# A recurrence and an expert layer on one core: the floor of the decay product inside its scan, a product moved to GpSimd, and one step in three rebalanced between TensorE and VectorE

## The chip, the cores and the metric

The kernel runs on one core of a Trainium2 chip. The metric is the device time of one execution in microseconds (us), taken as the median of several runs. The kernel before took 398.53 us (three runs, 396.94 to 400.71).

## What is computed

A decayed linear attention (4 batches, 8 heads, 768 tokens, 48 channels) feeds a layer of eight experts, of which each token takes one.

```python
for t in range(S):
    kt, vt, rt, wt = (k[:, :, t], v[:, :, t], r[:, :, t], w[:, :, t])
    cur = np.einsum('bhd,bhe->bhde', u[None] * kt, vt)
    y[:, :, t] = np.einsum('bhd,bhde->bhe', rt, state + cur)
    state = wt[:, :, :, None] * state + np.einsum('bhd,bhe->bhde', kt, vt)
...
e_idx = np.argmax(x @ w_gate, axis=1)
...
    h = np.maximum(x[mask] @ w1[e], 0.0)
    out[mask] = gate_w[mask, None] * eom[mask, e, None] * (h @ w2[e])
```

The term `cur` is the **own term** below: what a token takes from its own key and value, through u.

## The kernel before

**Two parts.** The recurrence is cut into 24 chunks of 128 tokens, six to a batch. It fills the first 152 us or so. Then come the experts, whose products fill TensorE almost to the end. The weights of the experts are fetched from about 125 us on, into five buffers.

**A unit** is the decay work for one or two chunks; there are 13 (units 0 and 1 have one chunk, unit u from 2 on has chunks 2(u-1) and 2(u-1)+1). All of it is on VectorE: `suffix` (L343) scans the decays w backwards into `sf` (L351), takes the whole product of a chunk from its first column, not less than FLOOR (2^-100), into `prods` (L357), and writes its reciprocal into the start of the next scan (L359). `times_rk` (L325) multiplies r and k into `rkp` (L331), for the own term. `prefix` (L361) scans forward into `pp` (L367). `scale_r` (L378) multiplies r by `pp` (L382) and `scale_k` (L371) k by `sf` (L375), both **in place** in the tile `rks`. So `scale_r` of a unit may only start when its `times_rk` has read r.

**A chunk.** TensorE forms the scores (`scores`, `pat`, L451). ScalarE copies them out, one instruction for each of two halves (L469); GpSimd puts the causal mask on each half (L475). In one chunk of three, from chunk 6 on, VectorE does copy and mask of one half in one instruction (L466). `outputs` (L536) sums masked scores times v (L550) and r times the old state (L558) in PSUM tile `py`, of which there is one buffer. `state` (L503) adds the old state to the new products on TensorE through a product with the identity (L509), or leaves that to VectorE (`tmp`, L525); ScalarE then scales the sum by `prods` into the next state (L530). `own` (L489) makes the own term `dv` on ScalarE (L494). It is added in one of two ways: by TensorE, through a product with the identity (L562), after which VectorE sums the gate columns (L593) and ScalarE copies the rows (L594, which waits for L593); or by VectorE (`sums`, L598 to L601, four instructions), which then frees `py` itself.

**Order.** Every engine works through its instructions in program order. That order comes from a table O of due times, in chunks. The entries `eu`, `ps` and `po` say where work goes, by u or k modulo 3: a positive `eu` puts `times_rk` on GpSimd, a positive `ps` adds the old state on TensorE, a positive `po` adds the own term on TensorE. `po` counts from chunk 6 on, and both end at chunk 17.

**After the recurrence** the rows of the last chunk are stored, and the next weights are queued behind that store on SyncE; the last tokens are routed, and GpSimd gathers their rows.

Of the kernel before, what the change touches and what calls it, by code (L numbers as in the profile page):

```python
# [17 lines left out]
ALU = mybir.AluOpType  # L18
# [33 lines left out]
FLOOR = 2.0 ** -100  # L52
# [1 line left out]
LIMIT = 2.0 ** 20  # L54


O = {'turnl': 0.22, 'fetch2': 1.36, 'fetch1': 1.35, 'fetch0': 1.34, 'list': 0.84, 'count': 0.83, 'match': 0.305, 'known': 0.839, 'read': -0.7, 'late': 0.46, 'vgm': -1.61, 'vgt': -1.07, 'vg': -1.618, 'vgo': -0.703, 'score': -1.649, 'so0': -1.336, 'so1': -1.268, 'mask0': -0.673, 'mask1': -0.914, 'key': -1.529, 'ko': -1.232, 'own': -0.619, 'state': -0.175, 'sto': -0.036, 'out': 0.238, 'sums': 0.397, 'const': 2.67, 'ra': 0.72, 'rd': 0.15, 'rb': 1.282, 'lr': [0, 22], 'lp': 2, 'pf': 0, 'rn': 5, 'rz': .45, 'rdz': 0.05, 'sumz': 0.323, 'sc': 2.6, 'scw': 0.9, 'open': -0.6, 'fetch': 3.4, 'up': 2.11, 'lo': 2.5, 'turn0': 4.3, 'turno0': 4.32, 'turn1': 4.301, 'turno1': 4.33, 'turn2': 4.302, 'turno2': 4.34, 'warm': 15, 'sc1': 1.55, 'sc2': [1.55, 1.55, 3.4, 3.4, 4.4, 4.4], 'ra2': .55, 'rd2': .07, 'rb2': 1.0, 'sc3': 5.939, 'lw': -5.962, 'lrk': -4.5, 'lv': -4.4, 'sfx': -3.687, 'pfx': -3.529, 'sk': -2.206, 'sr': -2.924, 'ruk': -3.598, 'min': 0.313, 'ed': 1, 'eu0': -1, 'ek0': -1, 'er0': -1, 'em00': -1, 'em01': 1, 'eu1': -1, 'ek1': -1, 'er1': -1, 'em10': 1, 'em11': 1, 'eu2': -1, 'ek2': -1, 'er2': -1, 'em20': 1, 'em21': 1, 'ps0': -1, 'po0': 1, 'ps1': 1, 'po1': -1, 'ps2': 1, 'po2': 1, 'ps3': 1, 'po3': 1, 'ps4': 1, 'po4': -1, 'sa0': 1, 'sa1': -1, 'sa2': 1, 'du': -1.35, 'raws': -.35, 'w0': 4, 'w1': 0, 'wt0': 0.945, 'wn0': 0, 'wt1': -1.03, 'wn1': 6, 'wt2': -0.602, 'wn2': 0, 'wt3': 1.387, 'wn3': 0}


@with_exitstack  # L60
def tile_rwkv_moe(ctx: ExitStack, tc, rkT, wz, v_tok, vT, r_raw, k_raw, v_raw,
                  w_raw, u, uT, wg, wgb, wog, w12, out):
    nc = tc.nc
    const = ctx.enter_context(tc.tile_pool(name="const", bufs=1))
# [86 lines left out]
    raws, pieces, nth = {}, {}, {}  # L151
# [165 lines left out]
    def load_rk(u):  # L317

        marks("lrk", u)
        k, n = units[u]  # L320
        rks[u] = pa.tile([P, 2 * NP, 2, C], F32, tag="rks", name="rks", bufs=RKB)
        nc.sync.dma_start(rks[u][:, 0:n * NP].rearrange("p n k t -> p (n k t)"),
                          rkT[k // 2, :, k % 2 * NP * 2 * C:][:, 0:n * NP * 2 * C])

    def times_rk(u, i=0):  # L325

        marks("rk", u, "lrk", i=i)
        n = parts(u, i) if u else slice(0, NP)
        if i == 0:
            rkp[u] = pa.tile([P, 2 * NP, C], F32, tag="rkp", name="rkp", bufs=2)  # L330
        engine(O["eu%d" % (u % 3)]).tensor_tensor(  # L331
            out=rkp[u][:, n], in0=rks[u][:, n, 0], in1=rks[u][:, n, 1], op=ALU.mult)

    def parts(u, i):

        if u == SPLIT:
            return slice(i * NP, (i + 1) * NP)
        return (slice(0, 2), slice(2, NP))[i] if u == 0 else slice(0, units[u][1] * NP)

    def flat(t, n):  # L340
        return t[:, n].rearrange("p n t -> p (n t)")

    def suffix(u, i=0):  # L343

        n = parts(u, i)
        marks("sfx", u, "lw", i=i)
        if u > 1:
            mark(("sfx", u, "dp", i), ("pfx", sum(units[u - 2]) - 1))
        if i == 0:
            sfs[u] = pa.tile([P, 2 * NP, W1C], F32, tag="sf", name="sf", bufs=2)  # L350
        nc.vector.tensor_tensor_scan(  # L351
            out=flat(sfs[u], n)[:, ::-1],
            data0=wts[u][:, n.stop * W1C:n.start * W1C:-1],
            data1=flat(dsx, n)[:, ::-1],
            initial=0.0, op0=ALU.mult, op1=ALU.add)
# [15 lines left out]
    def scale_k(u, i=0):  # L371
        n = parts(u, i)
        marks("sk", u, "sfx", "rk", i=i)
        kh = rks[u][:, n, 1]
        engine(O["ek%d" % (u % 3)] if u else -1).tensor_tensor(  # L375
            out=kh, in0=kh, op=ALU.mult, in1=sfs[u][:, n, 1:W1C])

    def scale_r(u, i=0):  # L378
        n = parts(u, i)
        marks("sr", u, "pfx", "rk", i=i)  # L380
        rh = rks[u][:, n, 0]
        engine(O["er%d" % (u % 3)] if u else -1).tensor_tensor(  # L382
            out=rh, in0=rh, op=ALU.mult, in1=pps[u][:, n, 0:C])
# [50 lines left out]
    def vgate_out(k):  # L434
# [547 lines left out]
    load_w(2)  # L982
    load_v(1)
    load_rk(2)
    nc.vector.memset(dsx, 0.0)
    nc.vector.memset(dsx[:, :, C], 1.0)
    nc.vector.memset(dpx[0], 0.0)
    make_identity(nc, ident)
    nc.gpsimd.memset(dpx[1], 0.0)
    constants()  # L990
    suffix(0, 0)
    prefix(0, 0)
    suffix(0, 1)
# [519 lines left out]
```

## Time and profile before

| what | value |
|---|---|
| median of 3 runs | 398.53 us (396.94 to 400.71) |
| profiled execution, its own time | 400.15 us |
| its span, first to last instruction | 398.6 us |
| TensorE busy in the span | 377.1 us (95%) |
| VectorE busy | 315.9 us (79%) |
| ScalarE busy | 245.7 us (62%) |
| GpSimd busy | 209.0 us (52%) |
| granted TensorE clock, mean | 0.993 |

Busy is the time in which at least one instruction of an engine ran. An instruction that waits inside its own duration, as for a port, counts as busy there. PE is TensorE's products, PEld its weight loads, DVE VectorE, ACT ScalarE, POOL GpSimd, SP SyncE. A row of the timeline gives start, duration, engine, line, operation, out<-in with shapes, and in brackets the idle time ahead of it with what ended it; "x2" is two instructions in a row.

### The profile page before, as it was taken

Reading aid. Unit: us, or ns where it says so; the run is one execution under the profiler, and the core shown is the slowest. Engines: PE = TensorE matmul, PEld = TensorE weight load, DVE = VectorE, ACT = ScalarE, POOL = GpSimd, SP = SyncE. Lnnn points to the kernel's source line nnn. Section 1 sums busy time; section 2 is a strip of 40 time slices with the busy share of each in tenths; the row PEclk is TensorE's granted clock in tenths of the full one; section 3 lists DMA queues with packets and bytes.
Section 4 is the critical chain, followed back from the end, with each engine's and each line's share of the span. In section 5 each row is a group of like instructions: output and inputs, shape, how many; then the busy total and the mean of one; then the engine's idle time right before and its main releaser. Section 6 shows DMA issues by size and latency. Waiting matters only on the chain.

```text
span 398.6 us, 10773 instructions
## 1 busy us (share of the span) xinstructions
PE 377.1 (95%) x4079; PEld 336.6 (84%) x4082; DVE 315.9 (79%) x616; ACT 245.7 (62%) x674; POOL 209.0 (52%) x234
## 2 busy tenths in 40 slices
PE   8899999999989998979999999999999999999992
PEld 3576788778767888879888999999999999999991
DVE  7999999999999877654777588699798798977521
ACT  1786789889797895422465485476556846666200
POOL 8614535668585585452053008617748388362723
PEclk9999999999999999999999999999999999999998
DMA  7995787998895822563449669789699798975212
GB/s 238 333 342 185 235 277 228 243 270 228 226 277 199 291 89 46 139 202 133 144 150 253 184 113 239 270 140 287 191 205 294 195 249 259 184 266 151 57 35 58
DMA packets 64936, 80.75 MB, mean 203 GB/s; under 512 B 40741, under 2 KB 49153, under 8 KB 63468
## 3 DMA queue, kind: packets, MB, share of 16 engines
q1 hardware_dynamic: 59580, 69.39, 62.3%
q0 software_dynamic: 4896, 10.34, 8.2%
q8 instruction: 34, 0.56, 0.6%
q10 hardware_dynamic: 400, 0.25, 0.2%
q14 instruction: 26, 0.21, 0.2%
HBM read 61.66 MB, written 10.30 MB: 181 GB/s over the span
## 4 chain that ended last, share of the span: by engine, by line
PE 56%; DVE 21%; issue 7%; DMA 6%; ACT 5%; POOL 2%; POOLq 1%; SPq 1%; ACTq 0%; DVEq 0%
PE ph L724 19%; PE acc L747 18%; DVE sf L351 3%; PE pat L451 3%; PE py L550 3%; DVE pp L367 3%; DMA raw<-in_w_dram 2%; PE py L562 2%; DVE wlo L172 2%; PE py L558 2%; DVE rkp L331 2%; PE pg L419 2%; DVE rks L375 2%; DMA xg<-xd,ids 2%; ACT whi L167 1%
## 5 line engine op out<-in xcount | busy, mean ns | idle before, releaser
L172 DVE TENSOR_TENSOR wlo<-raw,whi 128x768 fp32r<-128x768 f32 x64 | 64.0, 1000 | 20.9 <-ACT whi L167 20.1
L475 POOL TENSOR_SCALAR_AFFINE_SELECT a<-a 128x512 f32<-128x512 f32 x42 | 50.0, 1209 | 49.1 <-ACT a L469 49.1
L724 PE MATMUL ph<-xh,whi 128*128 128x384 f32 (+7 forms) x216 | 73.4, 340 | 0.8 <-DVE hl L730 0.4
L724 PE MATMUL ph<-xh,wlo 128*128 128x384 f32 (+7 forms) x216 | 72.8, 337 | 0.4 <-DVE wlo L172 0.4
L724 PE MATMUL ph<-xl,whi 128*128 128x384 f32 (+7 forms) x216 | 72.6, 336 | 0.2 <-DVE xl L939 0.2
L702 POOL COPY yj<-yr 112x384 uint16<-112x384 uint16 (+1 forms) x48 | 41.2, 912 | 57.6 <-DMA yr<-yp 57.6
L729 ACT ACTIVATE hh<-ph 128x384 fp32r<-128x384 f32 (+7 forms) x72 | 34.4, 479 | 48.9 <-PE ph L724 48.9
L747 PE MATMUL acc<-hh,whi 128*128 128x336 f32 (+6 forms) x168 | 58.7, 349 | 0.0
L747 PE MATMUL acc<-hl,whi 128*128 128x336 f32 (+6 forms) x168 | 58.5, 348 | 0.1
L747 PE MATMUL acc<-hh,wlo 128*128 128x336 f32 (+6 forms) x168 | 58.4, 347 | 0.0
L167 ACT CAST whi<-raw 128x768 fp32r<-128x768 f32 x62 | 51.8, 835 | 8.2 <-DMA raw<-in_w_dram 5.6
L730 DVE SCALAR_TENSOR_TENSOR hl<-ph,hh 128x384 fp32r<-128x384 f32 (+7 forms) x72 | 38.6, 538 | 17.4 <-ACT hh L729 17.3
L494 ACT ACTIVATE dv<-vt,dg 128x56 f32<-128x56 f32 x192 | 47.5, 354 | 0.4
L616 POOL DMA_INDIRECT xg<-xd,idm x28 | 30.1, 1073 | 25.6 <-issue 16.8
L675 POOL DMA_INDIRECT out_dram<-yo,idm x28 | 32.6, 1164 | 20.6 <-DVE yo L673 15.7
L724 PEld LDWEIGHTS ph<-xh,whi 128*128 128x128 f32 x216 | 40.8, 189 | 2.3 <-ACT xh L632 0.5
L724 PEld LDWEIGHTS ph<-xh,wlo 128*128 128x128 f32 x216 | 40.7, 188 | 1.4 <-DVE wlo L172 0.7
L724 PEld LDWEIGHTS ph<-xl,whi 128*128 128x128 f32 x216 | 40.7, 188 | 1.1 <-DVE xl L939 0.4
L268 POOL DMA_INDIRECT slot_table<-pair,slots x24 | 33.3, 1387 | 10.1 <-DVE lt L584 4.0
L747 PEld LDWEIGHTS acc<-hl,whi 128*128 128x128 f32 x168 | 31.9, 190 | 1.2 <-DVE hl L730 0.4
L747 PEld LDWEIGHTS acc<-hh,whi 128*128 128x128 f32 x168 | 32.1, 191 | 0.7
L747 PEld LDWEIGHTS acc<-hh,wlo 128*128 128x128 f32 x168 | 32.0, 190 | 0.7
(193 smaller groups left out, 764.4 us busy)
## 6 DMA issues: line engine op xcount, KB each, us to landing
raw<-in_w_dram SPq DMA_DIRECT2D x64, 384.0 KB
rks<-in_rkT_dram SPq DMA_DIRECT2D x11, 1024.0 KB
wts<-in_wz_dram SPq DMA_DIRECT2D x11, 516.5 KB
vt<-in_v_tok_dram SPq DMA_DIRECT2D x24, 224.0 KB
vs<-in_vT_dram SPq DMA_DIRECT2D x24, 192.0 KB
xd<-xt SPq DMA_DIRECT2D x24, 192.0 KB
wo<-in_wog_dram SPq DMA_DIRECT2D x8, 192.0 KB
rks<-in_rkT_dram SPq DMA_DIRECT2D x2, 512.0 KB
```

The lines of the kernel that those rows point to most:

```text
L167: (copy or nc.scalar.copy)(hi, raw)
L172: nc.vector.tensor_tensor(out=lo, in0=raws[e, f], in1=hi.bitcast(F32), op=ALU.subtract)
L268: nc.gpsimd.indirect_dma_start(out=tabs[i], out_offset=bass.IndirectOffsetOnAxis(ap=slots[:, i:i + 1], axis=0), in_=pair[:, i, :], in_offs ...
L475: nc.gpsimd.affine_select(out=a, in_=a, pattern=[[0, NP], [1, C]], compare_op=ALU.is_gt, fill=0.0, base=0, channel_multiplier=-1)
L494: nc.scalar.activation(out=dvs[k][:, p, o], in_=vts[k][:, p, VX * o:VX * o + VX], func=AF.Copy, scale=dgs[k][:, p, o:o + 1])
L616: nc.gpsimd.indirect_dma_start(out=xg[:, j, :], out_offset=None, in_=xd[0:rows, :], in_offset=bass.IndirectOffsetOnAxis(ap=idt[:, 2 * j:2 ...
L675: nc.gpsimd.indirect_dma_start(out=outs[view], out_offset=bass.IndirectOffsetOnAxis(ap=idt[:, 2 * j:2 * j + 1], axis=0), in_=yo, in_offset ...
L702: nc.gpsimd.tensor_copy(to[:, q], by[:, q])
L724: nc.tensor.matmul(ph[:, 0:nt], a[:, d * P:(d + 1) * P], x[:, d, 0:nt], start=k == 0, stop=k == 8)
L729: nc.scalar.activation(out=hh[:, 0:nt], in_=ph[:, 0:nt], func=AF.Relu)
L730: nc.vector.scalar_tensor_tensor(out=hl[:, 0:nt], in0=ph[:, 0:nt], scalar=0.0, in1=hh[:, 0:nt].bitcast(F32), op0=ALU.max, op1=ALU.subtract)
L747: nc.tensor.matmul(y[:, 0:nt], w[:, DM + i * P:DM + (i + 1) * P], a[:, 0:nt], start=start, stop=stop)
```

## The change

Four edits, all in the recurrence:

1. The scan `sf` takes the larger of its running product and a floor (`max` in place of `add`); the tile `dsx` holds FLOOR where it held 0. The `max` on VectorE (L357) goes; the reciprocal reads `sf`; a copy into `prods` follows, on GpSimd from unit 3 on, on VectorE before.
2. `times_rk` of units 4, 7 and 10 goes to GpSimd.
3. The own term of chunks 6, 9, 12 and 15 is added by VectorE (chunks 7, 10, 13, 16, 21, 22 and 23 were already).
4. The old state of chunks 3, 9 and 15 is added by TensorE.

```diff
-... 'eu1': -1, ... 'ps0': -1, 'po0': 1, ...
+... 'eu1': 1, ... 'ps0': 1, 'po0': -1, ...
...
-        engine(O["eu%d" % (u % 3)]).tensor_tensor(
+        engine(O["eu%d" % (u % 3)] if u > 3 else -1).tensor_tensor(
             out=rkp[u][:, n], in0=rks[u][:, n, 0], in1=rks[u][:, n, 1], op=ALU.mult)
...
-            initial=0.0, op0=ALU.mult, op1=ALU.add)
+            initial=0.0, op0=ALU.mult, op1=ALU.max)
         pc = prods[:, units[u][0] * NP + n.start:units[u][0] * NP + n.stop]
-        nc.vector.tensor_scalar(out=pc, scalar1=FLOOR, scalar2=None, op0=ALU.max,
-                                in0=sfs[u][:, n, 0])
-        nc.vector.reciprocal(dpx[u % 2][:, n, 0], pc)
+        nc.vector.reciprocal(dpx[u % 2][:, n, 0], sfs[u][:, n, 0])
+        (nc.gpsimd if u > 2 else nc.vector).tensor_copy(pc, sfs[u][:, n, 0])
...
-    nc.vector.memset(dsx, 0.0)
+    nc.vector.memset(dsx, FLOOR)
```

GpSimd around unit 4, before. The tiles a_107 to a_112 are the score halves of three chunks in turn; here a_108 and a_107 are chunk 3, a_110 and a_109 chunk 4:

```order
L475 AFFINE_SELECT a_112<-a_112 128x512
L475 AFFINE_SELECT a_111<-a_111 128x512
L475 AFFINE_SELECT a_108<-a_108 128x512
L475 AFFINE_SELECT a_107<-a_107 128x512
L475 AFFINE_SELECT a_110<-a_110 128x512
```

GpSimd at the same place, of the change:

```order
L474 AFFINE_SELECT a_112<-a_112 128x512
L474 AFFINE_SELECT a_111<-a_111 128x512
L474 AFFINE_SELECT a_108<-a_108 128x512
L358 COPY prods<-sf 128x8
L474 AFFINE_SELECT a_107<-a_107 128x512
L331 TENSOR_TENSOR rkp<-rks 128x1024
L474 AFFINE_SELECT a_110<-a_110 128x512
```

The copy of unit 4 stands between the two masks of chunk 3, and the product of unit 4 behind both. At units 7 and 10 the chunk has one mask on GpSimd, and the product stands right behind the copy.

VectorE at unit 4, before:

```order
L351 SCALAR_TENSOR_TENSOR sf<-wts,dsx 128x1032
L357 TENSOR_SCALAR prods<-sf 128x8
L359 RECIPROCAL dpx_105<-prods 128x8
L593 TENSOR_REDUCE logit<-py 128x8
L331 TENSOR_TENSOR rkp<-rks 128x1024
L367 SCALAR_TENSOR_TENSOR pp<-wts,dpx_105 128x1032
L525 TENSOR_TENSOR tmp<-pkv,st_93 128x224
L382 TENSOR_TENSOR rks<-rks,pp 128x8x128
```

VectorE there, of the change:

```order
L351 SCALAR_TENSOR_TENSOR sf<-wts,dsx 128x1032
L357 RECIPROCAL dpx_105<-sf 128x8
L592 TENSOR_REDUCE logit<-py 128x8
L366 SCALAR_TENSOR_TENSOR pp<-wts,dpx_105 128x1032
L381 TENSOR_TENSOR rks<-rks,pp 128x8x128
```

Three instructions are gone between the two scans and behind them; the last row, `scale_r`, now waits for GpSimd's product.

GpSimd at unit 12, before (a_110 and a_109 are chunk 19):

```order
L870 MEMSET xg 112x1152
L475 AFFINE_SELECT a_110<-a_110 128x512
L475 AFFINE_SELECT a_109<-a_109 128x512
L268 DMA slot_table<-pair,slots 3712x2 x2
L475 AFFINE_SELECT a_112<-a_112 128x512
```

And of the change:

```order
L869 MEMSET xg 112x1152
L474 AFFINE_SELECT a_110<-a_110 128x512
L358 COPY prods<-sf 128x8
L474 AFFINE_SELECT a_109<-a_109 128x512
L268 DMA slot_table<-pair,slots 3712x2 x2
L474 AFFINE_SELECT a_112<-a_112 128x512
```

The copy of unit 12 stands between the two masks of chunk 19, so the second of them now follows the scan of unit 12.

## Rows read from the trace of the kernel before

**Rows 1.** Busy time by stretch: span, then PE, PEld, DVE, ACT, POOL; clock, DMA.

```profile
45.00:82.00 37.00, 36.77 (x780) 30.28 (x780) 35.73 (x57) 33.65 (x123) 19.90 (x16) 1.00 0.82 248
...
138.00:152.00 14.00, 14.00 (x332) 11.78 (x329) 7.93 (x21) 13.97 (x52) 11.14 (x12) 1.00 0.25 79
```

**Rows 2.** The chain that ended last, in order of time: start us, us, what.

```profile
82.53 1.13 DVE rkp L331
...
156.54 4.42 DMA raw<-in_w_dram
```

**Rows 3.** VectorE in order of time around unit 4: start us, us.

```profile
37.43 0.17 DVE L357 TENSOR_SCALAR prods<-sf 128x8 f32<-128x8 f32 x1
37.63 0.21 DVE L359 RECIPROCAL dpx<-prods 128x8 f32<-128x8 f32 x1
...
37.84 1.22 DVE L331 TENSOR_TENSOR rkp<-rks 128x1024 f32<-128x1024 f32 x1
38.97 2.30 DVE L367 TENSOR_TENSOR_SCAN pp<-wts,dpx 128x1032 f32<-128x1032 f32 x1
41.19 0.37 DVE L525 TENSOR_TENSOR tmp<-pkv,st 128x224 f32<-128x224 f32 x1
41.47 1.31 DVE L382 TENSOR_TENSOR rks<-rks,pp 128x1024 f32<-128x1024 f32 x1
...
42.84 1.51 DVE L375 TENSOR_TENSOR rks<-rks,sf 128x1024 f32<-128x1024 f32 x1
```

**Rows 4.** ScalarE and GpSimd in order of time, scores of chunk 3.

```profile
38.33 1.08 ACT L469 COPY a<-pat 128x512 f32<-128x512 f32 x2
...
39.48 3.79 POOL L475 TENSOR_SCALAR_AFFINE_SELECT a<-a 128x512 f32<-128x512 f32 x2 [5.38 <-ACT a L469]
```

**Rows 5.** Mask's durations (ns min/median/max); GpSimd and VectorE in order of time.

```profile
L475 POOL TENSOR_SCALAR_AFFINE_SELECT a<-a x42: 628/1079/2534, 12.9 to 150.6; 128x512 f32<-128x512 f32 x42
...
84.13 2.18 POOL L475 TENSOR_SCALAR_AFFINE_SELECT a<-a 128x512 f32<-128x512 f32 x1 [2.10 <-ACT a L469]
...
83.58 2.30 DVE L367 TENSOR_TENSOR_SCAN pp<-wts,dpx 128x1032 f32<-128x1032 f32 x1
...
60.22 0.20 DVE L236 TENSOR_TENSOR sl<-rk,limit 128x48 f32<-128x48 f32 x1
...
93.76 1.55 POOL L475 TENSOR_SCALAR_AFFINE_SELECT a<-a 128x512 f32<-128x512 f32 x1
...
94.75 0.63 DVE L236 TENSOR_TENSOR sl<-rk,limit 128x48 f32<-128x48 f32 x1
```

**Rows 6.** VectorE and TensorE in order of time, own term on VectorE.

```profile
115.32 0.22 DVE L598 TENSOR_REDUCE lt<-py 128x8 f32<-128x64 f32 x1 [0.27 <-PE py L558]
...
116.46 1.25 DVE L331 TENSOR_TENSOR rkp<-rks 128x1024 f32<-128x1024 f32 x1
...
81.05 0.23 DVE L598 TENSOR_REDUCE lt<-py 128x8 f32<-128x64 f32 x1 [0.56 <-PE py L558]
...
101.58 1.15 PE L550 MATMUL py<-vt,a 128*64 128x56 f32 x32 [0.93 <-DVE xt L601]
```

**Rows 7.** Groups of instructions, 14 to 152 us; line L357 over the span.

```profile
L562 PE MATMUL py<-dv,ident 128*128 128x224 f32 x68 | 17.4, 379 | 0.0
...
L509 PE MATMUL pkv<-st,ident 128*128 128x224 f32 x26 | 7.5, 370 | 0.0
...
L530 ACT ACTIVATE st<-tmp,prods 128x56 f32<-128x56 f32 x12 | 3.1, 330 | 4.1 <-DVE tmp L525 4.1
...
L357 DVE TENSOR_SCALAR prods<-sf x15: 168/170/422, 4.5 to 130.3; 128x8 f32<-128x8 f32 x10, 128x4 f32<-128x4 f32 x3, 128x2 f32<-128x2 f32 x2
```

**Rows 8.** Routing, TensorE's outputs and GpSimd's masks of chunks 18 and 19.

```profile
123.81 0.20 DVE L203 TENSOR_TENSOR ohb<-io_m,em 128x48 bf16<-128x48 f32 x1
...
131.50 1.15 PE L550 MATMUL py<-vt,a 128*64 128x56 f32 x32 [0.33 <-ACT xt L594]
...
124.98 1.27 POOL L475 TENSOR_SCALAR_AFFINE_SELECT a<-a 128x512 f32<-128x512 f32 x2 [3.62 <-ACT a L469]
```

More of the change, by code (lines that the diff above doesn't have):

```diff
@@ L54 @@
 LIMIT = 2.0 ** 20
-O = {'turnl': 0.22, 'fetch2': 1.36, 'fetch1': 1.35, 'fetch0': 1.34, 'list': 0.84, 'count': 0.83, 'match': 0.305, 'known': 0.839, 'read': -0.7, 'late': 0.46, 'vgm': -1.61, 'vgt': -1.07, 'vg': -1.618, 'vgo': -0.703, 'score': -1.649, 'so0': -1.336, 'so1': -1.268, 'mask0': -0.673, 'mask1': -0.914, 'key': -1.529, 'ko': -1.232, 'own': -0.619, 'state': -0.175, 'sto': -0.036, 'out': 0.238, 'sums': 0.397, 'const': 2.67, 'ra': 0.72, 'rd': 0.15, 'rb': 1.282, 'lr': [0, 22], 'lp': 2, 'pf': 0, 'rn': 5, 'rz': .45, 'rdz': 0.05, 'sumz': 0.323, 'sc': 2.6, 'scw': 0.9, 'open': -0.6, 'fetch': 3.4, 'up': 2.11, 'lo': 2.5, 'turn0': 4.3, 'turno0': 4.32, 'turn1': 4.301, 'turno1': 4.33, 'turn2': 4.302, 'turno2': 4.34, 'warm': 15, 'sc1': 1.55, 'sc2': [1.55, 1.55, 3.4, 3.4, 4.4, 4.4], 'ra2': .55, 'rd2': .07, 'rb2': 1.0, 'sc3': 5.939, 'lw': -5.962, 'lrk': -4.5, 'lv': -4.4, 'sfx': -3.687, 'pfx': -3.529, 'sk': -2.206, 'sr': -2.924, 'ruk': -3.598, 'min': 0.313, 'ed': 1, 'eu0': -1, 'ek0': -1, 'er0': -1, 'em00': -1, 'em01': 1, 'eu1': -1, 'ek1': -1, 'er1': -1, 'em10': 1, 'em11': 1, 'eu2': -1, 'ek2': -1, 'er2': -1, 'em20': 1, 'em21': 1, 'ps0': -1, 'po0': 1, 'ps1': 1, 'po1': -1, 'ps2': 1, 'po2': 1, 'ps3': 1, 'po3': 1, 'ps4': 1, 'po4': -1, 'sa0': 1, 'sa1': -1, 'sa2': 1, 'du': -1.35, 'raws': -.35, 'w0': 4, 'w1': 0, 'wt0': 0.945, 'wn0': 0, 'wt1': -1.03, 'wn1': 6, 'wt2': -0.602, 'wn2': 0, 'wt3': 1.387, 'wn3': 0}
@@ new lines @@
+O = {'turnl': 0.22, 'fetch2': 1.36, 'fetch1': 1.35, 'fetch0': 1.34, 'list': 0.84, 'count': 0.83, 'match': 0.305, 'known': 0.839, 'read': -0.7, 'late': 0.46, 'vgm': -1.61, 'vgt': -1.07, 'vg': -1.618, 'vgo': -0.703, 'score': -1.649, 'so0': -1.336, 'so1': -1.268, 'mask0': -0.673, 'mask1': -0.914, 'key': -1.529, 'ko': -1.232, 'own': -0.619, 'state': -0.175, 'sto': -0.036, 'out': 0.238, 'sums': 0.397, 'const': 2.67, 'ra': 0.72, 'rd': 0.15, 'rb': 1.282, 'lr': [0, 22], 'lp': 2, 'pf': 0, 'rn': 5, 'rz': .45, 'rdz': 0.05, 'sumz': 0.323, 'sc': 2.6, 'scw': 0.9, 'open': -0.6, 'fetch': 3.4, 'up': 2.11, 'lo': 2.5, 'turn0': 4.3, 'turno0': 4.32, 'turn1': 4.301, 'turno1': 4.33, 'turn2': 4.302, 'turno2': 4.34, 'warm': 15, 'sc1': 1.55, 'sc2': [1.55, 1.55, 3.4, 3.4, 4.4, 4.4], 'ra2': .55, 'rd2': .07, 'rb2': 1.0, 'sc3': 5.939, 'lw': -5.962, 'lrk': -4.5, 'lv': -4.4, 'sfx': -3.687, 'pfx': -3.529, 'sk': -2.206, 'sr': -2.924, 'ruk': -3.598, 'min': 0.313, 'ed': 1, 'eu0': -1, 'ek0': -1, 'er0': -1, 'em00': -1, 'em01': 1, 'eu1': 1, 'ek1': -1, 'er1': -1, 'em10': 1, 'em11': 1, 'eu2': -1, 'ek2': -1, 'er2': -1, 'em20': 1, 'em21': 1, 'ps0': 1, 'po0': -1, 'ps1': 1, 'po1': -1, 'ps2': 1, 'po2': 1, 'ps3': 1, 'po3': 1, 'ps4': 1, 'po4': -1, 'sa0': 1, 'sa1': -1, 'sa2': 1, 'du': -1.35, 'raws': -.35, 'w0': 4, 'w1': 0, 'wt0': 0.945, 'wn0': 0, 'wt1': -1.03, 'wn1': 6, 'wt2': -0.602, 'wn2': 0, 'wt3': 1.387, 'wn3': 0}
```

## The prediction

> **What bounds the kernel now.** I read the busy time by stretch first. From 45 to 82 us TensorE is busy 36.77 of 37 us and VectorE 35.73 [rows 1]: two engines are full at once, and a microsecond taken from one is worth something only if the other keeps up. From 138 to 152 us VectorE has slack (7.93 of 14) and TensorE has none. The chain of waits tells which of the two decides: it runs through TensorE's steps until VectorE takes it over (the product r times k at 82.53 lies on it, [rows 2]), and is TensorE's again in the last stretch. What follows the recurrence hangs on its end: at 156.54 the chain goes through a weight transfer of 4.42 us [rows 2] that SyncE issues only behind the store of the last rows. So what the recurrence gains or loses arrives at the end in full.
>
> Two more things are to be seen. First, VectorE and GpSimd hold each other up. A mask alone takes 0.63 us; one that began at 84.13 took 2.18 and ended at 86.31, which is 0.43 after a VectorE scan that ran from 83.58 to 85.88 [rows 5]. So GpSimd stood until the scan was through and then needed 0.43 us for 512 elements. The other way, a small VectorE operation that takes 0.20 us took 0.63 beside a mask, and both ended at 95.3 to 95.4 [rows 5]. I read it so: a VectorE operation with two inputs in SBUF and a GpSimd operation that reads SBUF exclude one another, each for its whole length. Second, `scale_r` overwrites r, so it waits for the product r times k, wherever that is made.
>
> The Trainium skill, "SBUF — State Buffer", section "Who interferes with whom", says the same: a VectorE instruction with two SBUF inputs contends with a GpSimd instruction that reads SBUF, and the one that issues second blocks fully. The rows at 84.13 and 94.75 agree with it; it speaks against the second edit, and the sum below is what it would make of the time.
>
> **The change, part by part, on VectorE.**
>
> *Floor.* The `max` goes: from it to the reciprocal are 0.20 us (37.43 to 37.63, [rows 3]). Where GpSimd's mask runs then, it takes 0.42 instead of 0.17 [rows 7]; that happens in four of the units from 5 to 11 and saves 0.45 each there. Units 0 to 2 get a copy in its place: nothing. GpSimd's copy is new; a mask's 0.63 less the 0.43 it reads leaves 0.2 us for a tiny operation, my estimate. Between nothing and one whole mask (0.63) it changes little, except where a mask stands behind it (below).
>
> *Product.* VectorE loses 1.13 us for each of three (37.84 to 38.97, [rows 3]). No row shows this operation on GpSimd. It reads 2 x 1024 elements where the mask reads 512: four times 0.43 and 0.2 make 1.9 us. Lower bound: one mask alone, 0.63. Upper bound: four masks at their median under contention, 4 x 1.08 = 4.3 [rows 5]. I take 1.9, as the reading sets the hold. In that time VectorE can do nothing else here, since a scan and `scale_r` are all that come next, and both need the port or the product. So at units 7 and 10 it stands 1.9 us, whether the product gets in ahead of the scan `pp` or behind it.
>
> The Trainium skill, "GPSIMD Engine Reference", section "Performance versus the Vector engine", gives 4497 ns for a `tensor_tensor` of 2048 fp32 elements; half of that would be 2.25 us, an estimate, and the sum would grow by 0.35 for each product. No run here shows it.
>
> *Old state.* VectorE loses 0.28 us (41.19 to 41.47, [rows 3]) three times; ScalarE no longer waits for it, 4.1 us in all [rows 7].
>
> *Own term.* From the first of four instructions to the next other one are 1.14 us (115.32 to 116.46, [rows 6]), the middle of the five such places. What it replaces is one gate sum (L593): reciprocal and gate sum together take 0.21 (37.63 to 37.84, [rows 3]), of which I give it 0.14. So +1.0, four times.
>
> **Unit 4** needs its own working, as the product stands behind both masks of chunk 3. Before: `scale_r` at 41.47 [rows 3]. Now the scan ends 0.2 earlier (unit 3's floor), at 37.2; reciprocal and gate sum take 0.3, and `pp` runs 37.5 to 39.8. The two score copies, in before 38.33 to 39.41 [rows 4], come 0.3 earlier. The first mask waits for `pp` (in before it waited likewise: two masks took 3.79 us, [rows 4]) and ends at 40.2; copy 40.4; second mask 41.0; product 42.9. `scale_r` starts at 42.9: **1.4 late**, with two floors, the product and the old state already taken off.
>
> **The sum on VectorE**, from unit 3 to the routing of chunks 12 to 17 at 124 us:
>
> - up to `scale_r` of unit 4: +1.4
> - floors of units 5, 6, 8, 9 (0.45 each) and 11 (0.20): -2.0
> - units 7 and 10: -0.20 - 1.13 - 0.28 + 1.9 = +0.3 each: +0.6
> - own term of chunks 6, 9, 12, 15: +4.0
> - VectorE's waits for TensorE that a late VectorE no longer has, as 0.56 at 81.05 and 0.27 at 115.32 [rows 6], and two more: -1.4
> - `scale_k` ran 0.3 longer beside a mask (1.51 against the 1.22 of a product of the same shape, [rows 3]) in units 4, 7 and 10; the masks there now lie elsewhere: -0.9
>
> Together +1.7.
>
> **On TensorE** four chunks lose the own term, 17.4/17 = 1.02 us each, and three gain the old state, 7.5/13 = 0.58 each [rows 7]: -2.4, and some of its waits for ScalarE go. TensorE would be early, but it needs VectorE: for the routing (`ohb` at 123.81, [rows 8], is followed by TensorE's ranks and only then by the outputs of chunk 18), and for the outputs of chunk 19, which at 131.50 already waited 0.33 for the chain from VectorE's scan of unit 12 through L593 and ScalarE's copy [rows 8]. So TensorE's gain is lost in waiting. At chunk 19 there are +1.7, less unit 12's floor, 0.2: **+1.5**. Then TensorE works without a break, and the end moves by that.
>
> One wait is added there too: the second mask of chunk 19 was done at 126.25 [rows 8] and now follows the scan of unit 12, about 4 us later, the copy, and perhaps a whole VectorE operation that holds the port. It ends at about the time when the outputs start; behind it stand two routing scatters and the masks of chunk 20, which have 2 us to spare. I count it at nothing, with +1.0 as its upper end.
>
> The profiled execution, 400.15 us, would become 401.65. It lies 1.6 above the median of the runs shown, so on the median I forecast 398.53 + 1.5 = **400.0 us**.
>
> **Rivals.**
>
> *The port is shared, not held (faster).* If VectorE works on beside GpSimd's product, units 7 and 10 give -1.6 each, and only the masks delay unit 4 (+1.0). The sum is 1.0 - 2.0 - 3.2 + 4.0 - 1.4 - 0.9 = -2.5, and TensorE's own -2.4 would then be felt: 398.5 - 2.5 = 396.0. For it: GpSimd's spans are rough, and a mask is not a product. Against it: both blocked rows above. Chance 0.24.
>
> *The product is long (slower).* At 4.3 us the three products add 3 x 2.4 = 7.2 to the sum: about 407. From 2.8 us on (3 x 0.9 = 2.7 more) the kernel is slower by over 1%. For it: no row has a two-input operation on GpSimd, and masks under contention reach 2.53 us [rows 5]. Against it: that is waiting, not work. Chance 0.18, most of it near 403.
>
> *Nothing is felt,* because the weight transfer after the recurrence sets the next start: excluded by the chain, since its issue follows the last rows. The floor could also fail to save time, if the reciprocal just waits 0.42 where the `max` did; that costs 1.0 and lies inside the range.
>
> **How the numbers follow.** My forecast has 0.58 and by itself a range of 398.5 to 402.0. The faster rival reaches to 395.5, the slower one, but for its far end, to 403.5: the range is 395.5 to 403.5. About 1% is what a measurement of this kernel tells from no change: 394.5 and 402.5. Below lies only a faster rival that also keeps ScalarE's freed time: 0.12. Above lie the long product and a chunk 19 mask that is late as well: 0.18. The rest, 0.70, is within 1%.
>
> **What would show it.** GpSimd's product at 1.9 us after its port is free, never beside a two-input VectorE operation; VectorE idle some 3 us ahead of `scale_r` in unit 4 and about 2 in units 7 and 10; 1.1 us for each of the four new own terms; TensorE waiting for VectorE near chunks 13 to 19, with more idle time than before up to 131 us; the first weight transfer after the last rows at about 158 instead of 156.5 us. The prediction is wrong if VectorE's scans run on beside the product, or if TensorE's idle time shrinks.

## The result, and the profile after

The changed kernel takes 404.5 us (median of 4 runs, 403.78 to 404.67), the kernel before 397.9 us beside it (4 runs): a ratio of 1.0129, 95% interval 1.0085 to 1.0173. It is slower by 1.3%. A kernel's executions fall into a faster and a slower state, and the ratios here and below are taken in the faster one, so a ratio need not be the quotient of the two medians (1.0166 here). I had forecast 400.0 with a range up to 403.5, so 404.5 lies 1.0 us above the range. The sign of the forecast was right, the size and the mechanism were not.

| | before | after |
|---|---|---|
| median, us | 397.9 | 404.5 |
| profiled execution, us | 400.15 | 404.48 |
| span of its trace, us | 398.6 | 402.8 |
| mean granted clock | 0.993 | 0.977 |
| outputs of chunk 2 to those of chunk 18, us | 94.49 | 102.03 |

The last line is the stretch of the recurrence, from start to start, that holds nearly all that was changed; it serves as a measure below. The first view is the busy time by stretch (span, then PE, PEld, DVE, ACT, POOL; clock, DMA), which answers [rows 1]; first two stretches of the kernel before, then the changed kernel:

```profile
82.00:107.00 25.00, 23.44 (x475) 18.89 (x463) 24.66 (x42) 21.82 (x83) 16.44 (x12) 1.00 0.89 246
107.00:138.00 31.00, 29.49 (x599) 23.83 (x596) 29.77 (x55) 25.54 (x95) 20.43 (x15) 1.00 0.79 251
```

```profile
45.00:82.00 37.00, 34.91 (x745) 28.30 (x745) 36.46 (x55) 32.72 (x123) 23.02 (x19) 1.00 0.76 238
82.00:107.00 25.00, 22.24 (x414) 18.23 (x415) 23.45 (x40) 18.21 (x70) 16.57 (x14) 0.86 0.75 232
107.00:138.00 31.00, 26.83 (x506) 21.66 (x504) 26.09 (x49) 20.56 (x79) 20.28 (x17) 0.89 0.74 231
138.00:152.00 14.00, 14.00 (x312) 11.52 (x312) 11.64 (x15) 13.97 (x51) 12.41 (x10) 1.00 0.42 136
```

Up to 82 us this is as forecast: VectorE full, TensorE 1.9 us less busy than before. From 82 to 138 us it is not. VectorE, of which I expected that it would be the bound, is idle for 6.5 us there (1.6 before), and the granted clock, 1.00 in all of these stretches before, is 0.86 and 0.89. Neither VectorE nor TensorE is the bound, so I asked who is waited for. The group of TensorE's first output matmuls, 14 to 159 us (busy, mean ns | idle time ahead, and what ended it), says it in one line, first before, then after:

```profile
L550 PE MATMUL py<-vt,a 128*64 128x56 f32 x736 | 26.4, 224 | 1.8 <-DVE xt L601 0.9 <-ACT xt L594 0.5
```

```profile
L549 PE MATMUL py<-vt,a 128*64 128x56 f32 x736 | 28.0, 233 | 8.0 <-POOL a L474 6.4 <-DVE xt L600 1.0 <-ACT xt L593 0.4
```

TensorE waited 6.4 us for GpSimd's masks; in the kernel before not at all. It was in two places, chunk 11 and chunk 17. TensorE in order of time:

```profile
67.05 1.15 PE L549 MATMUL py<-vt,a 128*64 128x56 f32 x32 [0.99 <-DVE xt L600]
...
84.77 1.97 PE L549 MATMUL py<-vt,a 128*64 128x56 f32 x32 [2.34 <-POOL a L474]
86.67 1.12 PE L557 MATMUL py<-st,rks 64*64 64x56 f32 x32
87.72 1.86 PE L561 MATMUL py<-dv,ident 128*128 128x224 f32 x4
89.50 1.78 PE L450 MATMUL pat<-rks 64*128 64x128 f32 x16
...
123.25 1.96 PE L549 MATMUL py<-vt,a 128*64 128x56 f32 x32 [4.09 <-POOL a L474]
```

And GpSimd in order of time, ahead of the one and of the other:

```profile
71.09 2.36 POOL L331 TENSOR_TENSOR rkp<-rks 128x1024 f32<-128x1024 f32 x1
73.61 2.83 POOL L268 DMA_INDIRECT slot_table<-pair,slots  x1 [0.15 <-issue]
76.45 1.56 POOL L474 TENSOR_SCALAR_AFFINE_SELECT a<-a 128x512 f32<-128x512 f32 x2
78.18 1.78 POOL L268 DMA_INDIRECT slot_table<-pair,slots  x1 [0.16 <-issue]
79.97 1.77 POOL L474 TENSOR_SCALAR_AFFINE_SELECT a<-a 128x512 f32<-128x512 f32 x1
81.90 0.99 POOL L268 DMA_INDIRECT slot_table<-pair,slots  x1 [0.16 <-issue]
82.87 1.25 POOL L358 COPY prods<-sf 128x8 f32<-128x8 f32 x1
84.09 3.21 POOL L474 TENSOR_SCALAR_AFFINE_SELECT a<-a 128x512 f32<-128x512 f32 x2
...
107.60 0.19 POOL L358 COPY prods<-sf 128x8 f32<-128x8 f32 x1 [1.41 <-DVE sf L351]
...
118.77 0.65 POOL L474 TENSOR_SCALAR_AFFINE_SELECT a<-a 128x512 f32<-128x512 f32 x1
119.35 1.25 POOL L358 COPY prods<-sf 128x8 f32<-128x8 f32 x1
120.56 2.63 POOL L474 TENSOR_SCALAR_AFFINE_SELECT a<-a 128x512 f32<-128x512 f32 x1
```

From the product at 71.09 on GpSimd has no free moment up to 87.3 us, apart from some 0.15 us ahead of each scatter (the rows DMA_INDIRECT): product, scatter, two masks, scatter, first mask of chunk 11, scatter, copy, second mask (the first 0.62 us of the row at 84.09; the rest of that row is a mask of chunk 12). Only the second mask lets TensorE go on. At chunk 17 it is the same chain, and the mask there is held as well. Who holds copy and mask is seen on VectorE:

```profile
82.49 1.59 DVE L331 TENSOR_TENSOR rkp<-rks 128x1024 f32<-128x1024 f32 x1
...
119.17 1.38 DVE L331 TENSOR_TENSOR rkp<-rks 128x1024 f32<-128x1024 f32 x1
120.48 2.29 DVE L366 TENSOR_TENSOR_SCAN pp<-wts,dpx 128x1032 f32<-128x1032 f32 x1
...
128.09 0.22 DVE L592 TENSOR_REDUCE logit<-py 128x8 f32<-128x64 f32 x1 [3.60 <-PE py L561]
```

The copy of 8 elements takes 0.19 us alone (107.60) and 1.25 us at 119.35, since VectorE's product ran until 120.55; the mask that follows at 120.56 then finds the scan in its way, which began at 120.48 and ended at 122.77, and is through 0.43 us later. That is the mutual exclusion of [rows 5], now three links long: a tiny operation waits out one VectorE instruction, and the large one behind it in GpSimd's order has thereby lost its slot and waits out the next.

At the end of the recurrence the lateness is 6.4 us. The transfer of [rows 2] is issued here (SyncE's queue in order of time):

```profile
162.96 1.39 SPq L160 DMA_DIRECT2D raw<-in_w_dram  x3
```

That is 162.96 against 156.54. Of this 2.2 us do not arrive at the end of this pair of traces (spans 402.8 and 398.6), mostly because the profiled execution of the kernel before stood for a gather at 177.80 us, which the later TensorE of the changed kernel did not. It is the profiled execution of the kernel before, though, that lies 2.2 above its median; the medians differ by 6.6 us.

### The profile page after: what moved, and what is told of

Its sections match the earlier page's. It is cut to its first block, busy times and chain, and to the rows that moved or that the text cites. A ratio compares the mean times of both kernels' runs of the same rounds, so it can differ in the third digit from the quotient of the medians.

```text
span 402.8 us, 10765 instructions
## 1 busy us (share of the span) xinstructions
PE 377.5 (94%) x4069; PEld 337.1 (84%) x4072; DVE 317.2 (79%) x612; ACT 244.1 (61%) x670; POOL 224.4 (56%) x247
## 4 chain that ended last, share of the span: by engine, by line
PE 54%; DVE 15%; issue 8%; ACT 8%; POOL 7%; DMA 5%; SPq 1%; POOLq 0%; ACTq 0%; DVEq 0%
PE ph L723 17%; PE acc L746 16%; PE pat L450 4%; PE py L549 4%; DVE wlo L172 2%; ACT whi L167 2%; POOL a L474 2%; PE py L561 2%; PE py L557 2%; PE pg L418 2%; DMA raw<-in_w_dram 2%; DVE sf L351 2%; PE pkv L513 2%; PE pkt L482 1%; DMA yr<-yp 1%
## 5 line engine op out<-in xcount | busy, mean ns | idle before, releaser
L701 POOL COPY yj<-yr 112x384 uint16<-112x384 uint16 (+1 forms) x48 | 43.0, 948 | 57.9 <-DMA yr<-yp 57.9
L474 POOL TENSOR_SCALAR_AFFINE_SELECT a<-a 128x512 f32<-128x512 f32 x42 | 46.4, 1118 | 21.6 <-ACT a L468 21.5
L268 POOL DMA_INDIRECT slot_table<-pair,slots x24 | 36.3, 1512 | 9.4 <-issue 4.2
L549 PE MATMUL py<-vt,a 128*64 128x56 f32 x736 | 28.0, 233 | 8.0 <-POOL a L474 6.4
L549 PEld LDWEIGHTS py<-vt,a 128*64 128x64 f32 x736 | 25.0, 145 | 11.1 <-POOL a L474 7.6
L366 DVE TENSOR_TENSOR_SCAN pp<-wts,dpx 128x1032 f32<-128x1032 f32 (+2 forms) x15 | 33.8, 2252 | 0.0
```

Of the source, the lines that this page charges most:

```text
L268: nc.gpsimd.indirect_dma_start(out=tabs[i], out_offset=bass.IndirectOffsetOnAxis(ap=slots[:, i:i + 1], axis=0), in_=pair[:, i, :], in_offs ...
L366: nc.vector.tensor_tensor_scan(out=flat(pps[u], n), data0=wts[u][:, n.start * W1C:n.stop * W1C], data1=flat(dpx[u % 2], n), initial=0.0, o ...
L474: nc.gpsimd.affine_select(out=a, in_=a, pattern=[[0, NP], [1, C]], compare_op=ALU.is_gt, fill=0.0, base=0, channel_multiplier=-1)
L549: nc.tensor.matmul(py[o][t, p], at[k, o][:, p, t], vts[k][:, p, VX * o:VX * o + VX], start=p == 0, stop=False, skip_group_check=True)
L701: nc.gpsimd.tensor_copy(to[:, q], by[:, q])
```

## The experiments

My theory after the result: GpSimd's order of work is the cause. The product makes it late, the copy ahead of the second mask makes it lose a slot, TensorE stands at chunks 11 and 17, and its clock falls behind each stand. The rival is the recorded one: VectorE's sum, with four own terms at +4.0 us. The runs, as ratios to the kernel before on the same chip, with the stretch from chunk 2 to chunk 18 in the profiled execution (94.49 before):

| kernel | us | ratio, 95% | stretch, us |
|---|---|---|---|
| changed | 404.5 | 1.0129 (1.0085 to 1.0173) | 102.03 |
| a: product back on VectorE | 400.1 | 1.0020 (0.9996 to 1.0044) | 95.44 |
| b: copy on VectorE | 402.0 | 1.0073 (1.0043 to 1.0104) | 99.02 |
| e: copy behind the mask | 400.7 | 1.0046 (1.0021 to 1.0070) | 97.24 |
| j: filler in the stands | 401.4 | 1.0066 (1.0038 to 1.0094) | 99.12 |
| d: own term and old state back | 408.1 | 1.0228 (1.0194 to 1.0262) | 104.60 |
| h2: own term and old state alone | 399.4 | 0.9992 (0.9967 to 1.0016) | 95.62 |
| i2: product alone | 401.2 | 1.0042 (1.0017 to 1.0066) | 98.24 |
| g3: floor alone | 400.7 | 0.9964 (0.9931 to 0.9998) | 92.98 |

Four kernels (below as f, g2, h and i) ran on a chip on which the kernel before took 410.0 us, so that h, i and g2 were run once more elsewhere, as h2, i2 and g3.

**a. The product alone taken back.**

```diff
-... 'eu1': 1, ...
+... 'eu1': -1, ...
```

> The product of units 4, 7 and 10 goes back to VectorE; the floor, GpSimd's copy, the old state and the own term stay as changed. GpSimd-queue theory: its backlog at chunks 11 and 17 starts with the product (2.36 us each), so TensorE's stands of 2.34 and 4.09 us there shrink below 1 us each and the granted clock stays at 1.00 from 82 to 138 us; the shift of the recurrence (+6.4 us) falls to +1 to +2.5, the time to 398 to 400 us. If the copy's place alone makes the stands, they stay within 0.6 us and the time is 402 to 404. VectorE-sum theory (own terms +4.0 us, nothing from GpSimd's queue): the units lose 0.3 us each at most by the recorded sum, 0.6 by the measured 2.2 us hold, so the time stays at 402.5 to 404.

Measured: 400.1 us, at the upper end of what the theory of GpSimd's queue called for, ratio 1.0020; TensorE waits for no mask up to 145 us. GpSimd at chunk 11:

```profile
80.81 0.22 POOL L358 COPY prods<-sf 128x8 f32<-128x8 f32 x1
80.98 0.64 POOL L474 TENSOR_SCALAR_AFFINE_SELECT a<-a 128x512 f32<-128x512 f32 x1
```

Copy and mask stand in the same order as in the changed kernel, but they come 2.1 us earlier, ahead of VectorE's product, and take 0.22 and 0.64 us. So the copy does no harm where GpSimd is on time: the backlog that the product starts is needed. The rival, which had the time stay at 402.5 or more, is out. The clock did not stay at 1.00 all the way as expected (0.93 from 82 to 107 us): a wait of 1.23 us for VectorE at 86.03 is left.

**b. The copy on VectorE, the product left on GpSimd.**

```diff
-        (nc.gpsimd if u > 2 else nc.vector).tensor_copy(pc, sfs[u][:, n, 0])
+        nc.vector.tensor_copy(pc, sfs[u][:, n, 0])
```

> The copy of the suffix scan's first column runs on VectorE in all units; the product of units 4, 7 and 10 stays on GpSimd, as does the rest of the change. If the copy's place decides (it waits 1.25 us behind VectorE's product in front of the second mask, and the mask then falls behind a scan): the masks of chunks 11 and 17 come 1.3 and 3.3 us earlier, TensorE's stands fall under 1.2 us, no clock fall, time 399 to 400.5. If the product's backlog decides: the second mask of chunk 17 still begins at about 119.4 us and runs into the scan, stands of 1.5 and 3 us remain, time 402 to 403. VectorE-sum theory: VectorE gets 0.17 us for each of ten units more, time 405 to 406.

Measured: 402.0 us. GpSimd at chunk 17, and TensorE at chunk 14:

```profile
117.37 2.38 POOL L474 TENSOR_SCALAR_AFFINE_SELECT a<-a 128x512 f32<-128x512 f32 x2
```

```profile
104.29 1.72 PE L549 MATMUL py<-vt,a 128*64 128x56 f32 x32 [1.81 <-DVE xt L600]
```

Half of each reading came true. The stands at the masks are gone (0.56 us at chunk 11, nothing at chunk 17), as the copy's place would have it; both masks of chunk 17 go through from 117.37 on, one right behind the other, since no copy splits them. The time is still what I had written for the product's backlog. The loss now lies elsewhere: TensorE waits 1.81 us each at chunk 3 and chunk 14 for VectorE and ScalarE, with the lower clock behind the second (1.72 us for matmuls that take 1.15). The wait at chunk 3 is the product's hold on VectorE: the scan of unit 4 begins at 34.53 beside it, takes 4.46 us, and the gate sum that ScalarE and then TensorE wait for stands behind that scan. The wait at chunk 14 is not: the product of unit 10 begins only behind it, at 105.49, and the kernel h2 (below), which leaves the product on VectorE, waits as long there, against 0.93 in the kernel before [rows 6]. TensorE of h2:

```profile
102.33 1.15 PE L550 MATMUL py<-vt,a 128*64 128x56 f32 x32 [1.79 <-DVE xt L601]
```

It thus goes with the other place of own term and old state, which b and h2 share, and not with the product.

**e. The copy moved behind the second mask.**

```diff
-        (nc.gpsimd if u > 2 else nc.vector).tensor_copy(pc, sfs[u][:, n, 0])
+        if u < 4:
+            (nc.gpsimd if u > 2 else nc.vector).tensor_copy(pc, sfs[u][:, n, 0])
+
+    def product_out(u):
+        nc.gpsimd.tensor_copy(prods[:, units[u][0] * NP:sum(units[u]) * NP],
+                              sfs[u][:, 0:units[u][1] * NP, 0])
...
+        if m > 3:
+            when(k - 3.66, product_out, m)
```

> Only the place of GpSimd's copy changes: in units 4 and later it stands behind the second mask of its chunk instead of ahead of it; product, floor, old state and own term stay as changed. If the copy's place decides: the masks of chunks 11 and 17 come 1.3 and 3 us earlier, TensorE's stands of 2.34 and 4.09 us fall to about 1 us each, the granted clock does not fall behind them, time 399 to 400.5. If the product's backlog decides: stands of 1.5 and 3 us remain, time 402 to 403. VectorE-sum theory: nothing moves, 404 to 404.5.

Measured: 400.7 us, two thirds of the loss gone. GpSimd, then TensorE:

```profile
82.78 1.55 POOL L479 TENSOR_SCALAR_AFFINE_SELECT a<-a 128x512 f32<-128x512 f32 x1
...
119.67 2.19 POOL L362 COPY prods<-sf 128x8 f32<-128x8 f32 x1
```

```profile
84.39 1.15 PE L554 MATMUL py<-vt,a 128*64 128x56 f32 x32 [2.05 <-POOL a L479]
...
119.77 1.62 PE L554 MATMUL py<-vt,a 128*64 128x56 f32 x32 [2.03 <-POOL a L479]
```

The stand at chunk 17 falls from 4.09 to 2.03 us: the copy now waits 2.19 us behind the scan, and TensorE waits for nothing behind it. The 2 us that remain in both places are the product's backlog, as the mask at 82.78 runs into VectorE's product by itself. So each expectation was half right: of the two stands of the changed kernel (6.4 us) 2.3 go with the copy's place, and the other 4.1 I put down to the backlog.

**j. Is the clock a price of its own?** Matmuls that nothing reads were put into the two stands:

```diff
+    when(11 + O["out"] - .0001, warm, 9)
+    when(17 + O["out"] - .0001, warm, 16)
```

> The changed kernel with work added that nothing reads: 9 matmuls of 128 x 512 on TensorE just ahead of the outputs of chunk 11 and 16 ahead of those of chunk 17, about 2.0 and 3.5 us, which fit into the stands of 2.34 and 4.09 us there. If the fall of the granted clock behind the stands is a price of its own (the outputs were another 2.7 and 2.3 us later one chunk on): the clock stays at 1.00 in both places, the recurrence ends about 5 us earlier, time 399.5 to 401.5. If the stands themselves are the whole price: 404 to 405.

Measured: 401.4 us, inside what the clock's price called for. TensorE in order of time, and the busy time by stretch:

```profile
83.64 2.10 PE L969 MATMUL pw<-idle 128*128 128x512 bf16 x9 [0.19 <-DVE xt L600]
85.85 1.15 PE L549 MATMUL py<-vt,a 128*64 128x56 f32 x32
86.92 0.69 PE L557 MATMUL py<-st,rks 64*64 64x56 f32 x32
87.54 1.02 PE L561 MATMUL py<-dv,ident 128*128 128x224 f32 x4
88.50 1.23 PE L450 MATMUL pat<-rks 64*128 64x128 f32 x16
...
123.63 1.15 PE L549 MATMUL py<-vt,a 128*64 128x56 f32 x32 [0.33 <-POOL a L474]
```

```profile
82.00:107.00 25.00, 22.56 (x436) 17.24 (x435) 24.66 (x44) 20.21 (x77) 20.11 (x15) 1.00 0.79 241
107.00:138.00 31.00, 30.42 (x589) 23.37 (x588) 28.36 (x50) 21.72 (x77) 21.84 (x18) 1.00 0.70 220
```

The masks come as late as in the changed kernel, the useful work still starts late, but the clock stays at 1.00 and the four steps behind the stand take 1.15, 0.69, 1.02 and 1.23 us instead of 1.97, 1.12, 1.86 and 1.78: 2.6 us less at one stand. In the time it is about 0.6%, half of the loss. The stretch is only 2.9 us shorter, not 5; in the changed kernel part of what the slow clock cost was probably made up for by later waits that vanished. (The profiled execution of j took 405.5 us, 4.2 more than its median; it has a further stand of 1.85 us at 150.52 us, behind three gathers of GpSimd, which lies outside the stretch.)

**d, h, h2. The own term and the old state (the swap, below).** Back in the changed kernel (d), and alone in the kernel before (h, h2):

```diff
 (d, from the changed kernel)          (h, h2, from the kernel before)
-... 'ps0': 1, 'po0': -1, ...          -... 'ps0': -1, 'po0': 1, ...
+... 'ps0': -1, 'po0': 1, ...          +... 'ps0': 1, 'po0': -1, ...
```

> Old state back on VectorE and own term back on TensorE in chunks 6, 9, 12 and 15 (as before the change); floor, GpSimd's copy and product stay. VectorE-sum theory: four own terms of 1.0 us leave VectorE, three old states of 0.28 come back, so the time falls by 3 to 4 us, to 400 to 401, and VectorE's scan of unit 12 comes 3 us earlier. GpSimd-queue theory: copy and product still lie ahead of the masks of chunks 11 and 17; TensorE's stands remain at 1.5 us and more with the fall of the granted clock behind them, and the time stays at 402 to 404.

> The kernel before with one edit: in one chunk of three TensorE takes the old state and VectorE the own term. VectorE-sum theory: four own terms of 1.0 us less three old states of 0.28, less waits that are absorbed: +1 to +3 us, time 400.5 to 402.5. The kernel with these two put back (408 us against 404.5) speaks for the other way: TensorE loses 2.4 us, VectorE has room for it, and the time is 396.5 to 399.

> The kernel before with the old state on TensorE and the own term on VectorE in one chunk of three, once more, as the first run had 3.8 us of issue stalls on TensorE that the kernel before does not have in its profile (0.1). VectorE-sum theory: VectorE is late by 1 to 3 us from chunk 11 on, the masks of chunks 11 and 17 wait for its scans, time 1 to 2% over the kernel before. If the issue stalls made the first run slow: within 0.5% of the kernel before.

Measured: d 408.1 us, above both expectations; h 415.0 us where the kernel before took 410.0 (1.0199, 1.0147 to 1.0252), h2 399.4, no difference. In h TensorE stood 3.7 us from 22 to 152 us for nothing that the trace shows, in small pieces such as this; the kernel before shows no such piece there, and h2 has 0.2 us:

```profile
116.48 0.39 PE L419 MATMUL pg<-vs,wgb_sb 96*32 96x128 f32 x3 [0.32 <-issue]
```

So h's loss does not come from its edit alone, and I rely on h2: the two edits lengthen the stretch by 1.1 us and the time by nothing that can be measured. My own sum for these two edits (four own terms, three old states, absorbed waits: 4.0 - 0.84 - 1.4 = 1.8) was near that. In the company of floor and product they even gain 1%. VectorE of d suggests why:

```profile
90.86 0.23 DVE L592 TENSOR_REDUCE logit<-py 128x8 f32<-128x64 f32 x1 [2.97 <-PE py L561]
```

With the masks late VectorE waits for TensorE (2.97 us at 90.86, 1.00 in the changed kernel at the same chunk), so TensorE is the one that is short, and the 2.4 us that the swap takes from it would be felt: the stretch of d is 2.6 us longer than that of the changed kernel, though its stands at the masks of chunks 11 and 17 are shorter (2.01 and 3.04 us). This rests on one trace. I had the 2.4 us down as lost in waiting.

**i, i2. The product alone.**

```diff
-... 'eu1': -1, ...
+... 'eu1': 1, ...
...
-        engine(O["eu%d" % (u % 3)]).tensor_tensor(
+        engine(O["eu%d" % (u % 3)] if u > 3 else -1).tensor_tensor(
```

> The kernel before with one edit: the product of units 4, 7 and 10 on GpSimd (max after the scan, old state and own term as before). GpSimd-queue theory: the backlog behind the 2.36 us product delays the second mask of chunks 11 and 17 by 1 to 3 us even without a copy in the queue, TensorE stands there, time 403 to 407. VectorE-sum theory: three units lose 0.3 to 0.6 us each less nothing, time 399 to 401.

> The kernel before with the product of units 4, 7 and 10 on GpSimd, once more for the same reason (1.75 us of issue stalls). GpSimd-queue theory: masks late at chunk 11 or 17, TensorE stands 1.5 us and more, clock falls, 1 to 2% over the kernel before. If the product alone does no harm and needs the copy beside it: within 0.5%.

Measured: i 411.7 against 410.0 (1.0106, 1.0049 to 1.0163), i2 401.2 (1.0042). Alone the product does harm, but in i2 less than half of what it does in company (0.4% against the 1.1% of run a), and not at the masks of chunks 11 and 17. In i it did: TensorE waited for a mask at chunk 11, and its clock fell, with no copy in GpSimd's queue:

```profile
87.98 1.97 PE L550 MATMUL py<-vt,a 128*64 128x56 f32 x32 [1.88 <-POOL a L475]
```

So the product's backlog can make such a stand without the copy; with it, in the changed kernel, the stands were longer (2.34 and 4.09 us). GpSimd, VectorE and TensorE of i2 at unit 4:

```profile
34.04 3.32 POOL L331 TENSOR_TENSOR rkp<-rks 128x1024 f32<-128x1024 f32 x1
```

```profile
35.07 4.46 DVE L351 TENSOR_TENSOR_SCAN sf<-wts,dsx 128x1032 f32<-128x1032 f32 x1
```

```profile
40.72 1.72 PE L550 MATMUL py<-vt,a 128*64 128x56 f32 x32 [2.32 <-ACT xt L594]
```

VectorE's scan, 2.3 us by itself, takes 4.46 beside the product, TensorE stands 2.32 us and its clock falls. This is the hold on VectorE that I had priced, at its full size and with the clock's price on top. With the copy in the queue, which waits for that scan, the product of unit 4 comes behind the scan (at 37.04 in the changed kernel), and this stand is gone there.

**g2, g3. The floor alone, and f. The best of the parts.** In g2 and g3 all entries of the table are those of before and only the scan's floor with its copy on GpSimd is kept; f is the changed kernel with the product back on VectorE and the copy behind the second mask (a and e together).

> The kernel before with one edit: the floor in the suffix scan, with its copy on VectorE in units 0 to 2 and on GpSimd from unit 3. By the recorded sum VectorE gains 0.45 us in four units and 0.2 in others, 2.0 to 2.4 us in all, of which TensorE, full as well, lets through 0 to 1.5: time 397 to 399.7. If the copy in front of the second mask makes stands by itself, without the product's backlog: 400.5 to 402.

> The kernel before with the floor in the suffix scan alone, once more. By the recorded sum VectorE gains 2.0 us, of which TensorE lets through 0 to 1.5: 0 to 0.4% under the kernel before. If the copy costs the masks what the floor saves: 0 to 0.5% over it.

> Floor, old state and own term as changed; the product of units 4, 7 and 10 back on VectorE, and GpSimd's copy behind the second mask of its chunk from unit 4 on. GpSimd-queue theory: no mask stands behind a product or a copy in any chunk, TensorE waits for no mask, and the time is 0.5 to 1 us under that with the product back alone (400.1): 398.5 to 399.8. VectorE-sum theory: as the product back alone, 400 to 401.

Measured: g2 406.8 against 410.0 (0.9979, 0.9929 to 1.0030), g3 400.7 against 400.1 in the medians, but a ratio of 0.9964 (0.9931 to 0.9998), with a stretch 1.5 us shorter; f 407.2 against 410.0 (0.9992, 0.9952 to 1.0032), inconclusive. The floor alone is the only version whose interval lies below 1 in one of its runs, and only just; medians and ratio of g3 point different ways, so that a gain is not shown.

Taken together: floor -0.4%, own term and old state -0.1%, product +0.4%, each alone; floor and product without the other two (d) +2.3%; all of them +1.3%. The parts do not add up, and it is floor and product that do not. Most of the difference is GpSimd's queue, which the floor's copy and the product share: taking the copy out of it, moving it behind the mask or taking the product out gives back 0.6, 0.8 and 1.1 of the 1.3%.

## Why the prediction was wrong, step by step

The sum had terms for VectorE and TensorE and none for GpSimd's own order at chunks 11 and 17; this is the step that failed, and TensorE stood 6.4 us there. The sign is partly luck: it came from the own term's +4.0, not from where the loss is.

- **The copy, 0.2 us, which "changes little, except where a mask stands behind it".** The 0.19 us alone was right (107.60), but I followed the exception at one mask only, chunk 19's. The copies of units 8 and 11 stand between the two masks of chunks 11 and 17, cost 1.25 us each there, and let the second mask of chunk 17 fall behind a scan (2.63 us). In b both stands are gone but for 0.56 us, in e the one at chunk 17 is halved.
- **The product, 1.9 us of hold, counted on VectorE alone.** Its size: 2.36 and 2.37 us on GpSimd, and VectorE's scan beside it takes 4.48 us at 107.81 (below) instead of 2.30 [rows 3], a hold of 2.2. The Trainium skill's "GPSIMD Engine Reference", section "Performance versus the Vector engine", led to an estimate of 2.25 us, and the trace agrees with that rather than with my 1.9. This term is 0.3 short per product and does not explain 5 us. What I left out is that the product also stands in GpSimd's order, ahead of a scatter and the masks behind it. Run a shows that this is the main part: without the product there 1.1% of the 1.3% are gone.
- **TensorE's clock.** No term of the sum had it. The stand at chunk 11 cost 2.34 us and then, by the rows at 84.77 to 89.50 against those of j, 2.6 us of slower matmuls.
- **VectorE's sum.** It was about right as long as TensorE kept up. The suffix scans of units 7 to 10 begin 0.7, 1.5, 2.1 and 2.1 us later than before, where the terms of the sum, added up to the same places, make about 1.2, 2.2, 1.2 and 1.7; units 11 and 12 begin 3.4 and 6.4 later, behind the stands. The +1.7 that it gave for chunk 18 became +6.8. Inside the sum unit 4 was off: `scale_r` began at 41.41, as before, instead of 1.4 later. The floors of the first units, which I had at nothing, brought everything forward by about 1 us (the floor alone, g3, does so too). And [rows 4], which I read as the scores of chunk 3, are chunk 4's: the masks of chunk 3 ran at 30.31 before. In the changed kernel the second of them was done at 37.08, and the product behind it had only the scan `pp` to wait out, until 39.23. VectorE stood 2.19 us there, not 3. With a first term 1.4 too high, the sum came near at unit 7 partly by luck: some other term was too low, and no run shows which.

GpSimd before, then GpSimd and VectorE of the changed kernel, in order of time, for the product and unit 4:

```profile
30.31 3.79 POOL L475 TENSOR_SCALAR_AFFINE_SELECT a<-a 128x512 f32<-128x512 f32 x2 [4.25 <-ACT a L469]
```

```profile
36.44 0.64 POOL L474 TENSOR_SCALAR_AFFINE_SELECT a<-a 128x512 f32<-128x512 f32 x1
37.04 4.34 POOL L331 TENSOR_TENSOR rkp<-rks 128x1024 f32<-128x1024 f32 x1
```

```profile
41.41 1.63 DVE L381 TENSOR_TENSOR rks<-rks,pp 128x1024 f32<-128x1024 f32 x1 [2.19 <-POOL rkp L331]
...
107.81 4.48 DVE L366 TENSOR_TENSOR_SCAN pp<-wts,dpx 128x1032 f32<-128x1032 f32 x1
```

- **The own term, +4.0, and TensorE's gain, "lost in waiting".** The size of the first was right, 1.0 to 1.25 us each, but it was not the harm: h2. The second was wrong in this kernel, by the trace of d: TensorE's 2.4 us are the likeliest reason why d is slower than the changed kernel.
- **The rivals.** The shared port is out: the scan that takes 4.48 us did not run on beside the product. The long product is out as well, at 2.37 us against the 2.8 from which it would have decided. The time came out where that rival's near end lay, by a mechanism that I had not named.
- **What would show it.** GpSimd's product never worked beside a two-input VectorE operation: right, though at unit 4 it waited for one inside its own 4.34 us. TensorE waiting for VectorE near chunks 13 to 19: wrong, it waited for GpSimd. More idle time of TensorE up to 131 us: right, for another reason. The first weight transfer at about 158: at 162.96.

## What to carry to other kernels

When an instruction is given to another engine, follow that engine's own order past it until the next instruction that somebody waits for, in every period and not in the one that looks tight; a tiny instruction counts as much as a long one if it can be shut out, since what stands behind it loses its slot too. A wait of the engine that matters is not worth its length alone: look at whether its matmuls behind such a wait are longer, and add that. And price edits in company: here parts of 0.4% and less alone made 1.3% together, and two of them 2.3%.

## What the runs showed of the hardware

- A GpSimd copy of 128 x 8 elements takes 0.19 us alone and 1.25 or 2.19 us when it meets a VectorE operation with two inputs in SBUF, so it waits until that one is through. The Trainium skill, "SBUF — State Buffer", section "Who interferes with whom", calls the shared port pair an exclusive lock and says that the order of issue decides who blocks; the rows agree, down to a copy of 8 elements a partition.
- Behind a stand of 2.34 or 4.09 us TensorE's granted clock was down from 2.4 to 1.2 GHz (1.00 from 45 to 82 us, 0.50 from 84.8 to 88.0 and from 123.3 to 127.0): the same matmuls took 1.97 and 1.96 us instead of 1.15. Work that nothing reads, in place of the stand, kept it at 2.4 GHz (j). It is not settled what decides: in e a stand of 2.05 us was followed by full speed at first (1.15 at 84.39) and one of 2.03 by 1.62 (119.77).
- On one chip TensorE stood 0.6 to 3.7 us between 22 and 152 us with nothing in the trace to wait for, against none to 0.5 in the profiled executions elsewhere, and the same kernels took 6 to 16 us longer there. What these stalls are was not found, and they are too short to explain all of that.
